# A two-layer attention and SwiGLU kernel: QKV projections staged through DRAM with halo rows, attention cores rescheduled

## The chip, the cores and the metric

The kernel runs on one core of a Trainium2 chip. The metric is the device time of one execution in microseconds (us), as the median of several runs. Engines in the profile: PE is TensorE (PEld its weight loads), DVE is VectorE, ACT is ScalarE, POOL is GpSimd, SP is SyncE. In the traces an instruction that waits holds up those that stand behind it in its engine's queue. At 429 to 448 us of the kernel before (the chain further down) the multiplies of a core, L142, wait 8.09 and 3.20 us for shifted rows; three gate multiplies L206, whose inputs TensorE and ScalarE had finished by 440.5 us, stand behind them in VectorE's queue and start at 447.49, 449.22 and 450.42.

## The reference

Two layers, each of attention and an MLP, on a sequence of 2048 rows of 1024 numbers in bfloat16, with 32 heads of 32. Attention looks at 8 keys per row, at distances 0, 2, 4, ... 14.

```python
def attention(x, wqkv, wo):                 # W, dil = 8, 2
    q, k, v = split_heads(x @ wqkv)
    idx = pos[:, None] - arange(W)[None, :] * dil
    kg, vg = k[idx], v[idx]                 # 8 shifted copies of the rows; masked where idx < 0
    attn = softmax(where(mask, einsum("bhsd,bhswd->bhsw", q, kg) * Dh**-0.5, -1e9))
    return einsum("bhsw,bhswd->bhsd", attn, vg) @ wo
def mlp(x, w1, w3, w2):                     # F = 3584
    return (silu(x @ w1) * (x @ w3)) @ w2
for _ in range(2):
    x = x + attention(layernorm(x), wqkv, wo)
    x = x + mlp(layernorm(x), w1, w3, w2)
```

## The kernel before

The rows are cut into 4 blocks of 512, so there are 8 stages (layer, block). Each partition holds 4 neighbouring rows of one parity. The attention of a stage is done in 4 groups of 8 heads: `q_unit` projects K, V and Q of a group on TensorE, ScalarE copies PSUM into a tile `U`, and DMAs shift K and V rows between partitions so that each partition also has the 7 rows ahead of its own ("halo"). `core` then does scores, softmax and the weighted sum on VectorE, some 23 us for a group. The cores of block i+1 are written into the gate and up matmuls of block i.

```python
CFG = dict(n_pairs=2, NW=8, NU=3, NT=3, q_pos=(0, 2, 4, 6))
...
def q_unit(i, g, xT):
    b = i % NB
    U = work.tile([P, UE, UC], BF16, name="U", tag="U", bufs=cfg["NU"])
    for part, e0 in ((1, K0 + HALO), (2, V0 + HALO), (0, Q0)):
        ...                                     # matmuls into psq (2 PSUM buffers)
        nc.scalar.copy(out=U[:, e0 + 2 * jp:e0 + 2 * jp + 2, :], in_=ps[:])
    kv = U[:, 0:2 * KE, :].rearrange("p (t e) c -> p t e c", t=2)
    for h0 in (0, 64):                          # own rows of partition p-1 and p-2 become p's halo
        nc.scalar.dma_start(out=kv[h0 + 1:h0 + 64, :, 3:7, :], in_=kv[h0:h0 + 63, :, 7:11, :])
        nc.scalar.dma_start(out=kv[h0 + 2:h0 + 64, :, 0:3, :], in_=kv[h0:h0 + 62, :, 8:11, :])
    ...                                         # halo of the block's first partitions: carry, through DRAM
    return U

def core(i, g, U, o):                           # VectorE, with one Exp on ScalarE
    for w in range(W):                          # L142
        nc.vector.tensor_tensor(out=prod[:, w, :]..., in0=U[:, Q0:Q0 + C, :],
                                in1=U[:, K0 + HALO - w:K0 + HALO - w + C, :], op=ALU.mult)
    ...                                         # tree of adds, mask, max, subtract
    nc.scalar.activation(out=ex[:], in_=lg[:], func=ACTF.Exp, scale=float(DH) ** -0.5)
    ...                                         # sum, reciprocal, V multiplies, tree into o

def f_gu(i, xT, hT, fp):                        # gate and up of 256 columns
    ...                                         # 8 matmuls into pg (L200), 8 into pu (L203)
        nc.scalar.activation(out=sg[:], in_=pg[:], func=ACTF.Silu)
        nc.vector.tensor_tensor(out=hT[:, ft, :], in0=pu[:], in1=sg[:], op=ALU.mult)   # L206

for i in range(NS):
    o_proj(i, otile.pop(i))
    xf = ln_T(b)
    for fp in range(FT // 2):
        if i + 1 < NS and g < NG and fp == cfg["q_pos"][g]:
            U = q_unit(i + 1, g, xq[i + 1])
            core(i + 1, g, U, otile[i + 1])     # directly behind its projection
            g += 1
        f_gu(i, xf, hT, fp)
    if i + 2 < NS:
        xq[i + 2] = ln_T((i + 2) % NB)
    f_w2(i, hT, last=(i >= NS - NB))
```

Tiles have dependencies tracked for them, and a scheduler lays out each engine's queue from a model of durations; how early it places work behind a DMA seems to follow from what it thinks that DMA takes (run 2 bears on this; it was not tested by itself).

## Time and profile before

| | before |
|---|---|
| median of the runs | 2055.3 us (16 runs, 2047.8 to 2063.0) |
| span of the profiled run | 2052.6 us |
| mean granted TensorE clock | 0.93 |
| TensorE busy, VectorE busy | 84%, 51% |
| VectorE waiting for shifted rows | 266.2 us |

A line of the waits view names an engine, the instruction that waited and what it waited for; then us in total, times and the longest one. These lines of the kernel before are from it:

```profile
DVE prod L142 <- DMA U<-U: 266.2, 57, 11.5
...
PE pmm L200 <- DVE hT L206: 160.3, 27, 8.5
```

Fifty-seven waits, none over 11.5 us: the cores stand again and again, a little each time. One such chain, from the chain of work that ended last (start, length, what):

```profile
429.13 14.09 DMA U<-U
...
443.35 1.91 DVE prod L142 x3
...
447.49 0.69 DVE hT L206
...
448.23 3.57 PE pmm L200 x8
```

Read it downward: the shift lands, the core's multiplies start, the gate multiply L206 that stands behind them in VectorE's queue runs, and only then does TensorE get a PSUM buffer for the next gate matmuls, which take 3.57 us for eight, where an undisturbed group takes 1.89 us: about half the clock (granted 0.50 from 448.23 to 451.80 us, 1.00 from 315.34 to 350 us).

### The profile page before, as it was taken

How to read it: one execution, taken by the hardware profiler on the slowest of the kernel's cores; microseconds unless marked ns; L12 is line 12 of the kernel's file. 1: busy time of each engine (PE TensorE's matmuls, PEld its weight loads, DVE VectorE, ACT ScalarE, POOL GpSimd, SP SyncE). 2: the span in 40 equal slices, each digit the busy share in tenths (PEclk: the TensorE clock that was granted, in tenths of full speed). 3: DMA queues.
4: the chain of work that ended last, by engine and by line, in shares of the span. 5: the costliest groups of instructions: out<-in, count | busy, mean ns of one | idle time of the engine just before them, and what ended most of it. 6: DMA issues, size and time to landing. Idle time of an engine off the chain costs nothing.

```text
span 2052.6 us, 23292 instructions
## 1 busy us (share of the span) xinstructions
PE 1728.7 (84%) x9570; PEld 943.3 (46%) x9728; DVE 1048.7 (51%) x1562; ACT 457.7 (22%) x646; POOL 2.2 (0%) x9
## 2 busy tenths in 40 slices
PE   5618879987899878997889978898879978798998
PEld 4504534454445444454534545344544455444443
DVE  3885764256724567135861477515764246723111
ACT  2203222032211322122211322203222022211210
POOL 0000000000000000000000000000000000000000
PEclk9859989999899998999999989999989999999999
DMA  9403544445444444444454445444554544545452
GB/s 219 122 19 111 163 128 144 143 125 146 132 153 144 132 138 126 149 140 133 135 148 146 140 125 150 136 149 139 151 140 134 156 139 134 145 154 155 135 154 81
DMA packets 430715, 282.96 MB, mean 138 GB/s; under 512 B 8624, under 2 KB 418128, under 8 KB 430608
## 3 DMA queue, kind: packets, MB, share of 16 engines
q1 hardware_dynamic: 413184, 251.69, 42.7%
q10 hardware_dynamic: 17424, 29.77, 4.7%
q8 instruction: 76, 1.25, 0.2%
q14 instruction: 31, 0.25, 0.0%
HBM read 248.12 MB, written 4.60 MB: 123 GB/s over the span
## 4 chain that ended last, share of the span: by engine, by line
PE 63%; DMA 21%; DVE 9%; ACT 3%; issue 2%; ACTq 1%; SPq 0%; DVEq 0%
DMA U<-U 20%; PE pmm L217 19%; PE pmm L200 14%; PE psq L121 12%; PE pmm L203 11%; PE psq L188 5%; DVE prod L142 3%; DVE prod L147 2%; PE pt L107 1%; ACT U L123 1%; DVE hT L206 1%; ACT tT L108 1%; DVE prod L167 1%; ACT tT L182 1%; ACTq L134 1%
## 5 line engine op out<-in xcount | busy, mean ns | idle before, releaser
L200 PE MATMUL pmm<-tT,wpg 128*128 128x512 bf16 x1732 | 460.6, 406 | 186.2 <-DVE hT L206 160.3
L203 PE MATMUL pmm<-tT,wpg 128*128 128x512 bf16 x1749 | 432.6, 387 | 2.0
L121 PE MATMUL psq<-wpg,tT 128*128 128x256 bf16 x3072 | 366.8, 280 | 47.1 <-ACT U L123 47.1
L217 PE MATMUL pmm<-wpg,hT 128*128 128x512 bf16 x1753 | 388.0, 379 | 2.1
L200 PEld LDWEIGHTS <-wpg 128*128 128x128 bf16 x1792 | 182.8, 102 | 412.2 <-issue 233.7
L121 PEld LDWEIGHTS <-tT 128*128 128x128 bf16 x3072 | 308.3, 101 | 107.1 <-issue 50.7
L142 DVE TENSOR_TENSOR prod<-U 128x1024 bf16<-128x1024 bf16 x256 | 162.3, 687 | 353.3 <-DMA U<-U 266.2
L203 PEld LDWEIGHTS <-wpg 128*128 128x128 bf16 x1792 | 179.8, 100 | 225.3 <-issue 28.4
L217 PEld LDWEIGHTS <-hT 128*128 128x128 bf16 x1792 | 174.6, 98 | 207.2
L206 DVE TENSOR_TENSOR hT<-pmm,sg 128x512 bf16<-128x512 f32 x224 | 154.0, 687 | 216.5 <-PE pmm L203 198.4
L205 ACT ACTIVATE sg<-pmm 128x512 bf16<-128x512 f32 x224 | 131.6, 597 | 590.5 <-PE pmm L200 555.9
L221 DVE TENSOR_TENSOR x_sb<-pmm,x_sb 128x512 bf16<-128x512 f32 x64 | 44.3, 692 | 348.4 <-PE pmm L217 348.4
L123 ACT CAST U<-psq 128x512 bf16<-128x512 f32 x192 | 110.4, 585 | 268.8 <-PE psq L121 251.1
L167 DVE TENSOR_TENSOR prod<-U,a 128x1024 bf16<-128x1024 bf16 x256 | 157.0, 685 | 1.1
L147 DVE TENSOR_TENSOR prod<-prod 128x4096 bf16<-128x4096 bf16 (+3 forms) x128 | 153.4, 1198 | 1.4
L188 PE MATMUL psq<-wpg,tT 128*128 128x512 bf16 x496 | 111.7, 380 | 0.6 <-issue 0.2
L182 ACT COPY tT<-pt 128x1024 bf16<-128x1024 bf16 x32 | 30.2, 1025 | 341.0 <-PE pt L181 341.0
L97 DVE BATCH_NORM_STATS2 st<-x_sb 128x6 f32<-128x512 bf16 x128 | 82.0, 673 | 8.3 <-DMA x_sb<-in_A_x_dram 7.5
L205 ACT ACT_TABLE_LOAD x42 | 53.9, 1283 | 129.2 <-DMA carry<-U 40.3
L188 PEld LDWEIGHTS <-tT 128*128 128x128 bf16 x512 | 49.7, 98 | 57.5 <-issue 1.1
L170 DVE TENSOR_TENSOR prod<-prod 128x4096 bf16<-128x4096 bf16 x32 | 73.3, 2290 | 0.9
L108 ACT COPY tT<-pt 128x1024 bf16<-128x1024 bf16 x64 | 61.0, 1020 | 31.4 <-PE pt L107 31.4
(31 smaller groups left out, 444.2 us busy)
## 6 DMA issues: line engine op xcount, KB each, us to landing
wpg<-in_B_w_dram SPq DMA_DIRECT2D x336, 512.0 KB
wpg<-in_A_wqkv_dram SPq DMA_DIRECT2D x96, 512.0 KB
wpg<-in_A_wo_dram SPq DMA_DIRECT2D x32, 512.0 KB
U<-U ACTq DMA_DIRECT2D x64, 252.0 KB
U<-U ACTq DMA_DIRECT2D x64, 186.0 KB
x_sb<-in_A_x_dram SPq DMA_DIRECT2D x8, 512.0 KB
out_dram<-x_sb SPq DMA_DIRECT2D x8, 512.0 KB
carry<-U ACTq DMA_DIRECT2D x48, 8.0 KB
```

The source lines that it names most:

```text
L97: nc.vector.bn_stats(out=st[:, j, c, :], in_=x_sb[:, b * C + j, c * 512:(c + 1) * 512])
L121: nc.tensor.matmul(ps[:, jj, :], lhsT=xT[:, kt, j * P:(j + 1) * P], rhs=pg[:, kt, :], start=(kt == 0), stop=(kt == KT - 1))
L123: nc.scalar.copy(out=U[:, e0 + 2 * jp:e0 + 2 * jp + 2, :], in_=ps[:])
L142: nc.vector.tensor_tensor(out=prod[:, w, :].rearrange("p (j c) -> p j c", j=C), in0=U[:, Q0:Q0 + C, :], in1=U[:, K0 + HALO - w:K0 + HALO - ...
L147: nc.vector.tensor_tensor(out=pv[:, :, 0:n], in0=pv[:, :, 0:n], in1=pv[:, :, n:2 * n], op=ALU.add)
L167: nc.vector.tensor_tensor(out=pa[:, w, :].rearrange("p (g e t) -> p g e t", e=DH // 2, t=2), in0=U[:, V0 + HALO - w:V0 + HALO - w + C, :]. ...
L188: nc.tensor.matmul(ps[:], lhsT=oT[:, kt, j * P:(j + 1) * P], rhs=pgs[kt // 4][:, kt % 4, :], start=(kt == 0), stop=(kt == KT - 1))
L200: nc.tensor.matmul(pg[:], lhsT=w1p[:, kt, fi * P:(fi + 1) * P], rhs=xT[:, kt, :], start=(kt == 0), stop=(kt == KT - 1))
L203: nc.tensor.matmul(pu[:], lhsT=w3p[:, kt, fi * P:(fi + 1) * P], rhs=xT[:, kt, :], start=(kt == 0), stop=(kt == KT - 1))
L205: nc.scalar.activation(out=sg[:], in_=pg[:], func=ACTF.Silu)
L206: nc.vector.tensor_tensor(out=hT[:, ft, :], in0=pu[:], in1=sg[:], op=ALU.mult)
L217: nc.tensor.matmul(acc[j][:], lhsT=hT[:, ft, j * P:(j + 1) * P], rhs=pg[:, f4, :], start=(ft == 0), stop=(ft == FT - 1))
```

## The change

Its intent is to take the transfers of shifted rows off the path. The projections of all groups are written to DRAM (`kvd`, `qd`), and a group's K, V and halo come back with one wide load each, from three row offsets. The projection of a block is no longer tied to its cores: the four blocks of the first layer are projected up front, later ones in the tail of an MLP stage, three stages ahead. The cores get low priority, so that the scheduler spreads them among the gate multiplies. The diff, cut to its core:

```diff
+    kvd[(l, g)] = dram.tile([2, NCH, C * UC], BF16, ...)     # 4 leading rows of zeros
+    qd[(l, g)] = dram.tile([NB * P, C * UC], BF16, ...)
...
-                nc.scalar.copy(out=U[:, e0 + 2 * jp:e0 + 2 * jp + 2, :], in_=ps[:])
-        ... shifts U<-U and carries
+                nc.scalar.copy(out=stg[:, 2 * jp:2 * jp + 2, :], in_=ps[:])
+            src = stg[:].rearrange("p j c -> p (j c)")
+            if part == 0:
+                nc.scalar.dma_start(out=qd[(l, g)][b * P:(b + 1) * P, :], in_=src)
+            else:
+                nc.scalar.dma_start(out=kvd[(l, g)][part - 1, b * P + 4:(b + 1) * P + 4, :], in_=src)
+
+    def load_U(l, b, g):
+        U = work.tile([P, UE, UC], BF16, name="U", tag="U", bufs=cfg["NU"])
+        for t in range(2):
+            src = bass.AP(tensor=kv.tensor, offset=..., ap=[[row, P], [2 * row, 3], [1, row]])
+            nc.gpsimd.dma_start(out=U[:, t * KE:(t + 1) * KE, :]..., in_=src)
+        nc.gpsimd.dma_start(out=U[:, Q0:Q0 + C, :]..., in_=qd[(l, g)][b * P:(b + 1) * P, :])
...
+    def cores(s):
+        l, b = divmod(s, NB)
+        with tc.high_priority(offset=-cfg["bg"]):
+            otile[s] = work.tile([P, C, D], BF16, name="o", tag="o", bufs=cfg["NO"])
+            for g in range(NG):
+                U = load_U(l, b, g)
+                core(b, g, U, otile[s])
+
+    for b in range(NB):
+        xq = ln_T(b, per_tile=(b == 0))
+        for g in range(NG):
+            q_proj(0, b, g, xq)
+        if b == 0:
+            cores(0)
+    o_proj(0, otile.pop(0))
+    xf = ln_T(0)
     for i in range(NS):
...
+        if i + 1 < NS:
+            cores(i + 1)
+        if i >= 1 and (i - 1) + NB < NS:
+            xq2 = ln_T((i - 1) % NB)
         for fp in range(FT // 2):
-            if ...: U = q_unit(i + 1, ...); core(i + 1, ...)
-            f_gu(i, xf, hT, fp)
+            f_gu(xf, hT, fp)
+        if xq2 is not None:
+            for g in range(NG):
+                q_proj((i - 1) // NB + 1, (i - 1) % NB, g, xq2)
+        if i + 1 < NS:
+            o_proj((i + 1) % NB, otile.pop(i + 1))
+            xf = ln_T((i + 1) % NB)
+        f_w2(b, hT, last=(i >= NS - NB))
```

Also changed: neighbouring partitions now hold the two parities (the x loads step by two partitions), the first block's norm is done tile by tile, the output projection and norm of the next block move ahead of w2, and w_out pages are read once for all tiles.

More of the change, by code (lines that the diff above doesn't have):

```diff
@@ L25 @@
 NG = D // UC
-HALO = W - 1
-KE = HALO + C
+KE = 3 * C
+OWN = 2 * C
 K0, V0, Q0 = 0, KE, 2 * KE
 UE = 2 * KE + C
+NCH = 2 * (S // 2 // C) + 4
 EPS = 1e-5
 NEG = -1.0e9
-CFG = dict(n_pairs=2, NW=8, NU=3, NT=3, q_pos=(0, 2, 4, 6))
+CFG = dict(n_pairs=2, NW=8, NU=3, NT=3, NO=1, bg=4000)
 @with_exitstack
@@ L49 @@
     ps_tr = ctx.enter_context(tc.tile_pool(name="ps_tr", bufs=2, space=bass.MemoryType.PSUM))
-    ident = const.tile([P, P], BF16, name="ident")
-    make_identity(nc, ident[:])
-    mask = const.tile([P, W, C, HG], FP32, name="mask")
-    nc.gpsimd.memset(mask[:], 0.0)
-    for half in range(2):
-        sl = mask[half * 64:(half + 1) * 64]
-        nc.gpsimd.affine_select(out=sl, in_=sl, pattern=[[-1, W], [1, C], [0, HG]], compare_op=ALU.is_ge,
-                                fill=NEG, base=0, channel_multiplier=C)
-    x_sb = const.tile([P, NB * C, D], BF16, name="x_sb")
-    eps_t = const.tile([P, 1], FP32, name="eps_t")
-    nc.vector.memset(eps_t[:], EPS)
-    zero = const.tile([32, UC], BF16, name="zero")
-    nc.vector.memset(zero[:], 0.0)
-    zcarry = dram.tile([2, 2, 8, UC], BF16, name="zcarry")
-    nc.scalar.dma_start(out=zcarry[:].rearrange("a b e c -> (a b e) c"), in_=zero[:])
-    carry = {}
     xin = A_x[0].rearrange("(b q j two) d -> b two q j d", b=NB, q=64, j=C, two=2)
@@ L74 @@
     w2_v = B_w2.rearrange("(f p) n -> p f n", p=P)
+    x_sb = const.tile([P, NB * C, D], BF16, name="x_sb")
+    for b in range(NB):
+        for par in range(2):
+            nc.sync.dma_start(out=x_sb[par:P:2, b * C:(b + 1) * C, :], in_=xin[b, par])
+    zero = const.tile([64, 64], BF16, name="zero")
+    nc.vector.memset(zero[:], 0.0)
+    kvd = {}
+    qd = {}
+    for l in range(n_pairs):
+        for g in range(NG):
+            kvd[(l, g)] = dram.tile([2, NCH, C * UC], BF16, name=f"kvd{l}_{g}")
+            qd[(l, g)] = dram.tile([NB * P, C * UC], BF16, name=f"qd{l}_{g}")
+            for t in range(2):
+                nc.gpsimd.dma_start(out=kvd[(l, g)][t, 0:4, :].rearrange("r (s c) -> (r s) c", c=64), in_=zero[:])
+    ident = const.tile([P, P], BF16, name="ident")
+    make_identity(nc, ident[:])
+    eps_t = const.tile([P, 1], FP32, name="eps_t")
+    nc.vector.memset(eps_t[:], EPS)
+    mask = const.tile([P, W, C, HG], FP32, name="mask")
+    with tc.tile_pool(name="tmp", bufs=1) as tmp:
+        m0 = tmp.tile([64, W, C, HG], FP32, name="m0")
+        nc.gpsimd.memset(m0[:], 0.0)
+        nc.gpsimd.affine_select(out=m0[:], in_=m0[:], pattern=[[-1, W], [1, C], [0, HG]], compare_op=ALU.is_ge,
+                                fill=NEG, base=0, channel_multiplier=C)
+        for par in range(2):
+            nc.gpsimd.dma_start(out=mask[par:P:2], in_=m0[:])
     def page_cols(view, c0):
@@ L84, in page_rows, with ln_T @@
         return pg
-    for b in range(NB):
-        for par in range(2):
-            nc.sync.dma_start(out=x_sb[par * 64:(par + 1) * 64, b * C:(b + 1) * C, :], in_=xin[b, par])
-    def ln_T(b):
+    def ln_T(b, per_tile=False):
         xT = work.tile([P, KT, TB], BF16, name="tT", tag="tT", bufs=cfg["NT"])
@@ L94, in ln_T, with stats @@
         rs = work.tile([P, C], FP32, name="rs", tag="rs")
-        for j in range(C):
+        def stats(j):
             for c in range(2):
@@ L98, in ln_T, with rstd, norm @@
             nc.vector.bn_aggr(out=mv[:, j, :], in_=st[:, j, :, :])
-        nc.scalar.activation(out=rs[:], in_=mv[:, :, 1], func=ACTF.Sqrt, bias=eps_t[:, 0:1])
-        nc.vector.reciprocal(out=rs[:], in_=rs[:])
-        for j in range(C):
+        def rstd(j0, j1):
+            nc.scalar.activation(out=rs[:, j0:j1], in_=mv[:, j0:j1, 1], func=ACTF.Sqrt, bias=eps_t[:, 0:1])
+            nc.vector.reciprocal(out=rs[:, j0:j1], in_=rs[:, j0:j1])
+        def norm(j):
             xn = work.tile([P, D], BF16, name="xn", tag="xn")
@@ L108, in ln_T, with q_proj @@
             nc.scalar.copy(out=xT[:, :, j * P:(j + 1) * P], in_=pt[:])
-        return xT
-    def q_unit(i, g, xT):
-        b = i % NB
-        U = work.tile([P, UE, UC], BF16, name="U", tag="U", bufs=cfg["NU"])
-        for part, e0 in ((1, K0 + HALO), (2, V0 + HALO), (0, Q0)):
+        if per_tile:
+            for j in range(C):
+                stats(j); rstd(j, j + 1); norm(j)
+        else:
+            for j in range(C):
+                stats(j)
+            rstd(0, C)
+            for j in range(C):
+                norm(j)
+        return xT
+    def q_proj(l, b, g, xT):
+        for part in (1, 2, 0):
             pg = page_cols(wqkv_v, part * D + g * UC)
+            stg = work.tile([P, C, UC], BF16, name="stg", tag="stg", bufs=3)
             for jp in range(C // 2):
@@ L122, in q_unit, with core @@
                                          start=(kt == 0), stop=(kt == KT - 1))
-                nc.scalar.copy(out=U[:, e0 + 2 * jp:e0 + 2 * jp + 2, :], in_=ps[:])
-        kv = U[:, 0:2 * KE, :].rearrange("p (t e) c -> p t e c", t=2)
-        for h0 in (0, 64):
-            nc.scalar.dma_start(out=kv[h0 + 1:h0 + 64, :, 3:7, :], in_=kv[h0:h0 + 63, :, 7:11, :])
-            nc.scalar.dma_start(out=kv[h0 + 2:h0 + 64, :, 0:3, :], in_=kv[h0:h0 + 62, :, 8:11, :])
-        src = zcarry if b == 0 else carry[(i - 1, g)]
-        nc.scalar.dma_start(out=kv[0:P:64, :, 0:7, :], in_=src[:, :, 1:8, :])
-        nc.scalar.dma_start(out=kv[1:P:64, :, 0:3, :], in_=src[:, :, 5:8, :])
-        if b < NB - 1:
-            cr = dram.tile([2, 2, 8, UC], BF16, name=f"carry{i}_{g}")
-            carry[(i, g)] = cr
-            nc.scalar.dma_start(out=cr[:, :, 0:4, :], in_=kv[62:P:64, :, 7:11, :])
-            nc.scalar.dma_start(out=cr[:, :, 4:8, :], in_=kv[63:P:64, :, 7:11, :])
-        return U
-    def core(i, g, U, o):
-        b = i % NB
+                nc.scalar.copy(out=stg[:, 2 * jp:2 * jp + 2, :], in_=ps[:])
+            src = stg[:].rearrange("p j c -> p (j c)")
+            if part == 0:
+                nc.scalar.dma_start(out=qd[(l, g)][b * P:(b + 1) * P, :], in_=src)
+            else:
+                nc.scalar.dma_start(out=kvd[(l, g)][part - 1, b * P + 4:(b + 1) * P + 4, :], in_=src)
+    def load_U(l, b, g):
+        U = work.tile([P, UE, UC], BF16, name="U", tag="U", bufs=cfg["NU"])
+        kv = kvd[(l, g)]
+        row = C * UC
+        for t in range(2):
+            src = bass.AP(tensor=kv.tensor, offset=kv.offset + (t * NCH + b * P) * row, ap=[[row, P], [2 * row, 3], [1, row]])
+            nc.gpsimd.dma_start(out=U[:, t * KE:(t + 1) * KE, :].rearrange("p (r j) c -> p r (j c)", r=3), in_=src)
+        nc.gpsimd.dma_start(out=U[:, Q0:Q0 + C, :].rearrange("p j c -> p (j c)"), in_=qd[(l, g)][b * P:(b + 1) * P, :])
+        return U
+    def core(b, g, U, o):
         prod = work.tile([P, W, C * UC], BF16, name="prod", tag="prod", bufs=1)
@@ L142, in core @@
             nc.vector.tensor_tensor(out=prod[:, w, :].rearrange("p (j c) -> p j c", j=C), in0=U[:, Q0:Q0 + C, :],
-                                    in1=U[:, K0 + HALO - w:K0 + HALO - w + C, :], op=ALU.mult)
+                                    in1=U[:, K0 + OWN - w:K0 + OWN - w + C, :], op=ALU.mult)
         pv = prod[:].rearrange("p w (g d) -> p (w g) d", d=DH)
@@ L148, in core @@
             n //= 2
-        NL = W * C * HG
         lg = work.tile([P, W, C * HG], FP32, name="lg", tag="lg")
@@ L167, in core @@
             nc.vector.tensor_tensor(out=pa[:, w, :].rearrange("p (g e t) -> p g e t", e=DH // 2, t=2),
-                                    in0=U[:, V0 + HALO - w:V0 + HALO - w + C, :].rearrange("p j (h e t) -> p (j h) e t", e=DH // 2, t=2),
+                                    in0=U[:, V0 + OWN - w:V0 + OWN - w + C, :].rearrange("p j (h e t) -> p (j h) e t", e=DH // 2, t=2),
                                     in1=a2[:, w, :, :].unsqueeze(2).to_broadcast([P, C * HG, DH // 2, 2]), op=ALU.mult)
@@ L173, in core, with o_proj @@
                                 in1=pa[:, 1, :].rearrange("p (j c) -> p j c", j=C), op=ALU.add)
-    def o_proj(i, o):
-        b = i % NB
+    def o_proj(b, o):
         oT = work.tile([P, KT, TB], BF16, name="tT", tag="tT", bufs=cfg["NT"])
@@ L182, in o_proj @@
             nc.scalar.copy(out=oT[:, :, j * P:(j + 1) * P], in_=pt[:])
-        for ch in range(2):
-            pgs = [page_rows(wo_v, 4 * kh, ch * 512) for kh in range(2)]
-            for j in range(C):
+        pgs = [[page_rows(wo_v, 4 * kh, ch * 512) for kh in range(2)] for ch in range(2)]
+        for j in range(C):
+            for ch in range(2):
                 ps = ps_qo.tile([P, 512], FP32, name="psq", tag="psq")
                 for kt in range(KT):
-                    nc.tensor.matmul(ps[:], lhsT=oT[:, kt, j * P:(j + 1) * P], rhs=pgs[kt // 4][:, kt % 4, :],
+                    nc.tensor.matmul(ps[:], lhsT=oT[:, kt, j * P:(j + 1) * P], rhs=pgs[ch][kt // 4][:, kt % 4, :],
                                      start=(kt == 0), stop=(kt == KT - 1))
@@ L191, in o_proj, with f_gu @@
                 nc.vector.tensor_tensor(out=xs, in0=ps[:], in1=xs, op=ALU.add)
-    def f_gu(i, xT, hT, fp):
+    def f_gu(xT, hT, fp):
         w1p = page_cols(w1_v, fp * 256)
@@ L206, in f_gu, with f_w2 @@
             nc.vector.tensor_tensor(out=hT[:, ft, :], in0=pu[:], in1=sg[:], op=ALU.mult)
-    def f_w2(i, hT, last):
-        b = i % NB
+    def f_w2(b, hT, last):
         for ch in range(2):
@@ L223, in f_w2 @@
             for par in range(2):
-                nc.sync.dma_start(out=xout[b, par], in_=x_sb[par * 64:(par + 1) * 64, b * C:(b + 1) * C, :])
-    xq = {0: ln_T(0)}
-    otile = {0: work.tile([P, C, D], BF16, name="o", tag="o", bufs=2)}
-    for g in range(NG):
-        U = q_unit(0, g, xq[0])
-        core(0, g, U, otile[0])
-    if NS > 1:
-        xq[1] = ln_T(1 % NB)
+                nc.sync.dma_start(out=xout[b, par], in_=x_sb[par:P:2, b * C:(b + 1) * C, :])
+    otile = {}
+    def cores(s):
[5 more added lines that the diff above has]
+                core(b, g, U, otile[s])
+    for b in range(NB):
+        xq = ln_T(b, per_tile=(b == 0))
[5 more added lines that the diff above has]
+    xf = ln_T(0)
     for i in range(NS):
-        b = i % NB
-        o_proj(i, otile.pop(i))
-        xf = ln_T(b)
+        l, b = divmod(i, NB)
         hT = work.tile([P, FT, TB], BF16, name="hT", tag="hT", bufs=1)
         if i + 1 < NS:
-            otile[i + 1] = work.tile([P, C, D], BF16, name="o", tag="o", bufs=2)
-        g = 0
+            cores(i + 1)
+        xq2 = None
+        if i >= 1 and (i - 1) + NB < NS:
+            xq2 = ln_T((i - 1) % NB)
         for fp in range(FT // 2):
-            if i + 1 < NS and g < NG and fp == cfg["q_pos"][g]:
-                U = q_unit(i + 1, g, xq[i + 1])
-                core(i + 1, g, U, otile[i + 1])
-                g += 1
-            f_gu(i, xf, hT, fp)
-        if i + 2 < NS:
-            xq[i + 2] = ln_T((i + 2) % NB)
-        f_w2(i, hT, last=(i >= NS - NB))
+            f_gu(xf, hT, fp)
+        if xq2 is not None:
+            for g in range(NG):
+                q_proj((i - 1) // NB + 1, (i - 1) % NB, g, xq2)
[3 more added lines that the diff above has]
+        f_w2(b, hT, last=(i >= NS - NB))
 _INS = ['A_x', 'A_wqkv', 'A_wo', 'B_x', 'B_w1', 'B_w3', 'B_w2']
```

## The prediction

> **What bounds the kernel now.** I read the page first (busy shares and the 40 slices), then the chain that ended last, then the groups, then the timeline of TensorE in one stage.
>
> ```profile
> PE 1728.7 (84%) x9570; PEld 943.3 (46%) x9728; DVE 1048.7 (51%) x1562; ACT 457.7 (22%) x646; POOL 2.2 (0%) x9
> ...
> PEclk9859989999899998999999989999989999999999
> ...
> PE 63%; DMA 21%; DVE 9%; ACT 3%; issue 2%; ACTq 1%; SPq 0%; DVEq 0%
> ```
>
> TensorE is the busiest engine, but only 63% of the chain is its work: 21% is DMA, and the by-line row under it puts 20% on U<-U, the shift of K and V rows between partitions. A DMA stands in the chain only if work waits for it. The groups say who does:
>
> ```profile
> L200 PE MATMUL pmm<-tT,wpg 128*128 128x512 bf16 x1732 | 460.6, 406 | 186.2 <-DVE hT L206 160.3
> L142 DVE TENSOR_TENSOR prod<-U 128x1024 bf16<-128x1024 bf16 x256 | 162.3, 687 | 353.3 <-DMA U<-U 266.2
> L206 DVE TENSOR_TENSOR hT<-pmm,sg 128x512 bf16<-128x512 f32 x224 | 154.0, 687 | 216.5 <-PE pmm L203 198.4
> ```
>
> The attention core on VectorE (L142) waits 266.2 us for U<-U, the gate multiply (L206) stands behind it in the same in-order queue, and the gate matmul (L200) waits 160.3 us for L206 to free its PSUM buffer. So a late DMA stops TensorE through two in-order queues. Timeline of TensorE in the first stage (start, us, ..., idle before):
>
> ```profile
> 233.83 3.57 PE L200 MATMUL pmm<-tT,wpg 128*128 128x512 bf16 x8 [5.06 <-DVE hT L206]
> ...
> 267.19 3.57 PE L200 MATMUL pmm<-tT,wpg 128*128 128x512 bf16 x8 [5.52 <-DVE hT L206]
> ...
> 303.21 3.57 PE L200 MATMUL pmm<-tT,wpg 128*128 128x512 bf16 x8 [6.33 <-DVE hT L206]
> ...
> 315.34 1.89 PE L200 MATMUL pmm<-tT,wpg 128*128 128x512 bf16 x8
> 317.06 1.89 PE L203 MATMUL pmm<-tT,wpg 128*128 128x512 bf16 x8
> ```
>
> One stop per head group; after it, eight matmuls take 3.57 us (half clock); undisturbed, groups of eight start 1.725 us apart, 215.7 ns per matmul. The start is worst, as no MLP work exists yet beside block 0's cores. Windows of 50 us (PE, PEld, DVE, ACT, POOL busy, clock, DMA share, GB/s):
>
> ```profile
> 100.00:150.00 50.00, 2.07 (x18) 1.23 (x16) 46.20 (x62) 2.69 (x5) 0.00 (x0) 0.55 0.10 29
> 350.00:400.00 50.00, 49.04 (x248) 23.26 (x252) 5.53 (x8) 3.42 (x4) 0.00 (x0) 1.00 0.47 147
> ```
>
> The first shows TensorE empty while VectorE works alone; the second what a full TensorE looks like: clock 1.00, weights at 147 GB/s.
>
> **TensorE's floor.** N=512: 5376+512 = 5888 x 215.7 ns = 1270 us. N=256 (QKV): 3072 x 109 ns (48 in 5.25 us in the chain) = 335 us. Transposes: 768 x about 57 ns = 44 us. Sum about 1650 us; the span is 2052.6, so 403 us are idle or at half clock, close to the chain's 20.4% for U<-U (419 us).
>
> [...] 1.725 us per eight, 3.57 us after each 5 to 6 us stop. [...] the x loads into half tiles ran at 222 to 223 GB/s, the weights behind them at 290 to 294. [...]
>
> **The change part by part.**
>
> (1) U<-U and carries go. Instead each K, V, Q part is stored to DRAM (3 parts x 32 units = 96 stores of 256 KB, 25 MB) and U is loaded with its halo by GpSimd (K and V 768 KB each, Q 256 KB, 1.8 MB x 32 = 59 MB). About 30 MB of shifts leave, so traffic goes from 283 to about 335 MB: near 190 GB/s over a 1760 us span. The trace moved 290 GB/s at its fullest, so it fits on average.
>
> (2) All four layer-0 projections are done first, and later ones a stage or more ahead; cores run at low priority. A load of U then has tens of us of slack (three U buffers, one core 23.2 us). The built program's order shows cores spread between the gate multiplies, not in front of them. This removes the 266.2 us wait, and with it most of the 160.3 us and the half clock. VectorE work is unchanged: one core is 8x0.687 + 4.8 + 8x0.685 + 2.29 + 1.22 + 0.69 + 3.2 of small operations = 23.2 us; a stage has four (93), 28 gate multiplies (19), 16 residual adds (11) and one or two layer norms (8.5 each): 132 to 140 us. TensorE needs 164 us per stage, 206 with a projection. TensorE bounds.
>
> (3) The start. I expect the first QKV near 27 us (25.9 before). The first core needs three projections (11 us), a store and a load[...]: near 47 us. In the order the norm of block 2 stands inside the fourth core: 47 + 3x24 + 8 = 127 us on VectorE, while TensorE arrives at 27 + 84 = 111 us; it waits 16 us (partly sooner, as each Exp stands before PSUM copies in ScalarE's queue). Then two blocks of QKV (2x42) and their transposes: output projection at about 215 us. Projection 16 us, then norm and transposes with nothing else for TensorE, 14 us: the MLP starts at 245 us.
>
> (4) From there the remaining TensorE work is 1650 less 168 (QKV), 8 (norm transposes), 16 (projection) and 2: 1456 us, so 1701 us with no stop, and 8 us for the last adds and stores (TensorE ends at 2044.6 of 2052.6 now): 1709 us.
>
> (5) New stops. Between gate multiplies the order places 3.7 to 3.8 us of VectorE work where cores run, against TensorE's 3.45 us; PSUM gives about 5 us of slack. Stages 0 and 1 have no projection to catch up in: first gate of stage 0 to the thirteenth of stage 1 is 223 us of VectorE against 208 of TensorE: 10 us lost. Seven output projections: an add, a core multiply and a norm statistic per tile, 2.1 against 1.73 us: 2.5 us each, 17. Seven norms behind them: about 2 us each, 14. w2 drains and U arrivals: 10. Sum about 50. **1760 us.**
>
> **Rivals.** (a) GpSimd's loads come late[...]: the wait L142 <- U<-U returns as U<-kvd. For it: a load is four times the bytes of a shift and every load goes through an engine new to this. Against: loads are issued up to two cores ahead[...]. If each of 32 cores waited 5 us, half hidden: 1840. (b) VectorE's queue becomes the bound: its order comes from a model, and if it is some 5% too dense all along, 7 stages x 10 us more: 1830. For it: segments of 5.0 to 5.7 us in the order; against: VectorE is idle in the second half of stages 1 to 5. (c) DMA contention: while projections and cores overlap[...]. Then TensorE waits for weights at the start: 20 to 40 us, 1790. (d) Transfers were hidden anyway: refuted by the chain's 20%.
>
> **Range and chances.** The floor of start, 1650 and tail is 27+1650+8 = 1685, so under 1715 all would have to be hidden; (a), (b), (c) give 1790 to 1840. Range 1715 to 1835. Missing 2% (2015) would need more than 250 us of new waits: faster 0.98.
>
> **What would show it right or wrong.** Right: L164 (core multiply) idle for DMA under 60 us; L220 (gate) idle for L226 under 70; granted clock 0.97 or more; DMA gone from the chain save at the start; first gate matmul at 235 to 260 us; about 335 MB moved; GpSimd's loads never the releaser of a long wait in the middle. Wrong: waits on U<-kvd above 100 us (a), TensorE idle spread over all gate groups (b), TensorE idle for weight pages or PSUM copies behind a stage store (c), or a first gate matmul past 290 us.

The sum on record was 1760 us, with one cut term in it: in (3), about 9 us for a store and a load, an estimate given without its numbers, which leads from 27 and 11 to the 47 us and so into the 245 and the 1760. TensorE's paces are those of the trace: from 315.34 to 342.96 us 16 groups of eight start 1.726 us apart.

## The result, and the profile after

The changed kernel takes **1748.0 us** (median of 8 runs, 1744.1 to 1749.5) against 2055.3 us, and its output is correct. The ratio is 0.8502, 95% interval 0.8489 to 0.8515. (Ratios here are the mean time of one kernel's fast runs over that of the other's of the same rounds, so not quite the ratio of the medians quoted.) From the page of the changed kernel: engines, granted clock by slice, bytes moved, and the chain by engine.

```profile
PE 1666.4 (95%) x9597; PEld 926.7 (53%) x9728; DVE 1039.1 (60%) x1565; ACT 432.5 (25%) x624; POOL 76.5 (4%) x122
...
PEclk9899999999999999999999999999999999999999
...
DMA packets 443564, 337.36 MB, mean 193 GB/s; under 512 B 11040, under 2 KB 412704, under 8 KB 443456
...
PE 64%; DVE 30%; ACT 2%; DMA 2%; issue 2%; SPq 0%; POOL 0%; DVEq 0%; POOLq 0%; ACTq 0%
```

VectorE does the same work (1039 us against 1049) and TensorE is busy at 95%. DMA fell from 21% of the chain to 2%, although more bytes move (337.36 MB against 282.96). The groups that answer to the three shown before (line numbers differ: L220 is the gate matmul, L164 the core's first multiply, L226 the gate multiply):

```profile
L220 PE MATMUL pmm<-tT,wpg 128*128 128x512 bf16 x1751 | 424.4, 382 | 14.5 <-DVE x_sb L240 11.8
...
L226 DVE TENSOR_TENSOR hT<-pmm,sg 128x512 bf16<-128x512 f32 x224 | 154.1, 688 | 308.4 <-PE pmm L223 296.2
...
L164 DVE TENSOR_TENSOR prod<-U 128x1024 bf16<-128x1024 bf16 x256 | 161.9, 680 | 19.4 <-DMA U<-qd 18.8
```

The core waits 19.4 us for its inputs in place of 353.3 (266.2 of that for the shifts, 77.7 for PSUM copies), and the gate matmul 14.5 in place of 186. VectorE now waits for TensorE (308.4 us), as it should where TensorE bounds. The core's wait that is left is a single one, at the start, as the waits view shows:

```profile
POOL U L157 <- DVE prod L188: 1135.0, 27, 124.1
...
DVE prod L164 <- DMA U<-qd: 18.8, 1, 18.8
...
PE psq L142 <- ACT stg L144: 16.0, 4, 10.1
```

GpSimd, which issues the loads, stands 1135 us at full U buffers: the loads are ready to go before there is room. The same two windows as before (PE, PEld, DVE, ACT, POOL busy, clock, DMA share, GB/s):

```profile
100.00:150.00 50.00, 44.24 (x401) 38.72 (x400) 48.11 (x67) 17.73 (x29) 4.07 (x6) 0.97 0.85 269
350.00:400.00 50.00, 48.73 (x257) 23.38 (x260) 47.99 (x74) 9.57 (x11) 2.03 (x3) 1.00 0.60 191
```

In the first, TensorE was at 2.07 us before. In the second both engines are nearly full.

**Where the 307 us came from.** In the kernel before, the first w2 matmul is at 349.65 us, and the dense TensorE work done until then is about 202 us: some 148 us lost. In the changed kernel TensorE reaches the first gate matmul at 251.45 us after about 192 us of dense work: 59 lost. (Both sums of dense work are estimates from the paces in the prediction.) So the start gave about 88 us. From one w2 to the next, a stage took 246 to 249 us before (349.65, 595.43, 844.34). In the changed kernel a stage without a projection takes about 170 us, those with one 211.6 (517.57 to 729.15). The rest, about 220 us, came from the stages.

### The profile page after: what moved, and what is told of

Its sections match the earlier page's. It is cut to its first block, busy times and chain, and to the rows that moved or that the text cites. A ratio compares the mean times of both kernels' runs of the same rounds, so it can differ in the third digit from the quotient of the medians.

```text
span 1745.3 us, 23469 instructions
## 1 busy us (share of the span) xinstructions
PE 1666.4 (95%) x9597; PEld 926.7 (53%) x9728; DVE 1039.1 (60%) x1565; ACT 432.5 (25%) x624; POOL 76.5 (4%) x122
## 2 busy tenths in 40 slices
DMA packets 443564, 337.36 MB, mean 193 GB/s; under 512 B 11040, under 2 KB 412704, under 8 KB 443456
## 3 DMA queue, kind: packets, MB, share of 16 engines
q10 hardware_dynamic: 13824, 25.17, 3.8%
## 4 chain that ended last, share of the span: by engine, by line
PE 64%; DVE 30%; ACT 2%; DMA 2%; issue 2%; SPq 0%; POOL 0%; DVEq 0%; POOLq 0%; ACTq 0%
PE pmm L223 21%; PE pmm L220 21%; PE psq L142 13%; DVE prod L164 6%; PE pmm L236 6%; DVE prod L169 5%; DVE prod L188 5%; DVE st L106 3%; DVE prod L191 2%; DVE x_sb L211 2%; DVE x_sb L240 1%; PE psq L208 1%; DVE prod L192 1%; PE pt L119 1%; ACT tT L120 1%
## 5 line engine op out<-in xcount | busy, mean ns | idle before, releaser
L220 PE MATMUL pmm<-tT,wpg 128*128 128x512 bf16 x1751 | 424.4, 382 | 14.5 <-DVE x_sb L240 11.8
L223 PE MATMUL pmm<-tT,wpg 128*128 128x512 bf16 x1757 | 421.5, 380 | 2.8 <-DVE x_sb L240 0.8
L142 PE MATMUL psq<-wpg,tT 128*128 128x256 bf16 x3072 | 343.6, 275 | 16.5 <-ACT stg L144 16.0
L226 DVE TENSOR_TENSOR hT<-pmm,sg 128x512 bf16<-128x512 f32 x224 | 154.1, 688 | 308.4 <-PE pmm L223 296.2
L142 PEld LDWEIGHTS <-tT 128*128 128x128 bf16 x3072 | 303.4, 99 | 55.7 <-issue 17.3
L220 PEld LDWEIGHTS <-wpg 128*128 128x128 bf16 x1792 | 175.3, 98 | 225.2 <-issue 19.0
L223 PEld LDWEIGHTS <-wpg 128*128 128x128 bf16 x1792 | 175.7, 98 | 213.2 <-issue 4.0
L164 DVE TENSOR_TENSOR prod<-U 128x1024 bf16<-128x1024 bf16 x256 | 161.9, 680 | 19.4 <-DMA U<-qd 18.8
L144 ACT CAST stg<-psq 128x512 bf16<-128x512 f32 x192 | 112.0, 585 | 219.9 <-PE psq L142 218.0
L193 DVE TENSOR_TENSOR o<-prod 128x1024 bf16<-128x1024 bf16 x32 | 22.0, 686 | 231.7 <-PE pt L201 231.1
L157 POOL DMA_DIRECT2D U<-kvd x64 | 47.6, 744 | 1210.7 <-DVE prod L188 1135.0
L208 PEld LDWEIGHTS <-tT 128*128 128x128 bf16 x512 | 49.4, 98 | 56.6
L119 PE MATMUL pt<-ident,xn 128*128 128x128 bf16 x512 | 41.4, 235 | 34.7 <-DVE xn L115 33.5
```

The lines of the kernel that those rows point to most:

```text
L142: nc.tensor.matmul(ps[:, jj, :], lhsT=xT[:, kt, j * P:(j + 1) * P], rhs=pg[:, kt, :], start=(kt == 0), stop=(kt == KT - 1))
L144: nc.scalar.copy(out=stg[:, 2 * jp:2 * jp + 2, :], in_=ps[:])
L164: nc.vector.tensor_tensor(out=prod[:, w, :].rearrange("p (j c) -> p j c", j=C), in0=U[:, Q0:Q0 + C, :], in1=U[:, K0 + OWN - w:K0 + OWN - w ...
L208: nc.tensor.matmul(ps[:], lhsT=oT[:, kt, j * P:(j + 1) * P], rhs=pgs[ch][kt // 4][:, kt % 4, :], start=(kt == 0), stop=(kt == KT - 1))
L220: nc.tensor.matmul(pg[:], lhsT=w1p[:, kt, fi * P:(fi + 1) * P], rhs=xT[:, kt, :], start=(kt == 0), stop=(kt == KT - 1))
L223: nc.tensor.matmul(pu[:], lhsT=w3p[:, kt, fi * P:(fi + 1) * P], rhs=xT[:, kt, :], start=(kt == 0), stop=(kt == KT - 1))
```

## The experiments

All 12 outputs but that of `after_nocore` are correct. I had three theories of the main gain. DISTANCE: what cost was that a core is asked for directly behind the projection that feeds it. TRANSPORT: the wide loads through DRAM are what is faster than 64-partition shifts. PRIORITY: the low priority of the cores is what spreads them. Later, two theories of what sets the end of the start.

**1. DRAM staging kept, distance taken away.** Each group's projection goes back to directly ahead of its core, at the places that the kernel before used.

```diff
+    def unit(n, g, xq, o):
+        q_proj(l, b, g, xq); U = load_U(l, b, g); core(b, g, U, o)
...
-        if i + 1 < NS:
-            cores(i + 1)
         for fp in range(FT // 2):
+            if i + 1 < NS and g < NG and fp == (0, 2, 4, 6)[g]:
+                unit(i + 1, g, xq[i + 1], otile[i + 1]); g += 1
             f_gu(xf, hT, fp)
```

> The changed kernel with its DRAM staging and its loads, but the projections put back where the kernel before has them: each head group's projection directly ahead of its core, inside the MLP of the block before, core at ordinary priority. Theory DISTANCE (the gain comes from loading U long before its core is due): the wait returns as core multiply <- U<-qd, some 8 to 12 us per head group, 150 to 330 us over the run, and the time goes back to 1950 to 2080 us. Rival TRANSPORT (store plus load through DRAM is simply quicker or cheaper than the shift between partitions): at most 1850 us.

Measured: 1967.8 us (ratio to before 0.9577, 0.9548 to 0.9606), so 220 us of the 307 are lost again, inside what DISTANCE expected and far above the 1850 of TRANSPORT. Its waits and the window of the start:

```profile
DVE prod L164 <- DMA U<-qd: 206.0, 29, 27.6
```

```profile
100.00:150.00 50.00, 4.71 (x30) 3.29 (x32) 42.71 (x57) 4.68 (x6) 0.00 (x0) 0.51 0.00 0
```

The wait is back as U<-qd, now longer each time (up to 27.6 us), since a round trip is a store and a load (those of Q land in 5.5 and 4.7 us at the median); the start is empty again. Stages take 236.8 us. So DRAM staging without distance keeps about 88 us, together with the stride-two partitions and the shared w_out pages, which this run keeps too. The 220 us that went are not distance alone: the run also puts the output projection and norm back behind w2.

**2. Partition shifts kept, cores called later.** In the kernel before, each core is called two gate steps behind its projection.

```diff
-                U = q_unit(i + 1, g, xq[i + 1])
-                core(i + 1, g, U, otile[i + 1])
+                pend.append((g, q_unit(i + 1, g, xq[i + 1])))
...
+            if pend and fp == cfg["q_pos"][pend[0][0]] + 2:
+                gg, U = pend.pop(0)
+                core(i + 1, gg, U, otile[i + 1])
```

> The kernel before with its partition shifts kept and no DRAM staging, but each core called two MLP steps (about 14 us of gate and up matmuls) after its projection, so that the shift has time. Theory DISTANCE: the core's wait for U<-U (266 us) falls below 100 us and the time to 1790 to 1900 us; the start of the run stays as bad as before, so it does not reach 1748. Rival TRANSPORT: the shifts still block ScalarE's queue and arrive late, 1980 to 2060 us.

Measured: 1971.8 us (0.9585, 0.9557 to 0.9613), outside of what DISTANCE expected and a little under what the rival expected.

```profile
DVE prod L142 <- DMA U<-U: 185.1, 56, 11.1
...
PE pmm L200 <- DVE hT L206: 73.5, 25, 7.8
```

The 185.1 us show that no distance was made: there are still 56 waits. In the timeline most of a projection ran at 443.8 to 451.9 us, its shifts were issued at 449 to 455, and the core that uses them still began at 458.4, directly behind the core before it. Calling a core later in the program did not make it later in the queue here; presumably the scheduler put it where its model thought the rows would be there, which was not looked at. So this run decides nothing between the theories.

**3. Partition shifts kept, with real distance.** Three of the next block's four groups are projected ahead of the previous block's w2, into the three U buffers; the cores are called in the next stage.

```diff
+        us[i + 2] = [q_unit(i + 2, g, xq[i + 2]) for g in range(3)]     # ahead of f_w2
         f_w2(i, hT, last=(i >= NS - NB))
...
-                U = q_unit(i + 1, g, xq[i + 1])
-                core(i + 1, g, U, otile[i + 1])
+            if i + 1 < NS and fp in (0, 2, 4, 6):
+                g = fp // 2
+                core(i + 1, g, us[i + 1][g], otile[i + 1])
+                if g == 0:
+                    us[i + 1].append(q_unit(i + 1, 3, xq[i + 1]))
```

> The kernel before with its partition shifts kept (no staging through DRAM), but with real distance: the projections of groups 0 to 2 of the next block are made ahead of the previous block's w2, into three U buffers, and the cores are called during the gate and up of the next block. DISTANCE (what costs is that a core is asked for directly behind the projection that feeds it): the 266 us that VectorE waits for the shifted rows fall below 60 us, the stages after the first shorten from 246 us to 205-220 us, the start stays as it was, total 1800-1880 us. TRANSPORT (the DRAM staging with its wide loads is what is faster, whatever the order): the wait stays above 130 us and the total above 1930 us.

Measured: 1904.0 us (0.9251, 0.9235 to 0.9267), between the two expectations; the wait fell to 135.3 us, not below 60, and is just on TRANSPORT's side of the expected lines (above 130). In the timeline of TensorE, the stage from 383.5 to 618.6 us (235 us) has one long stop left in its gate matmuls, and three at the new place:

```profile
438.67 3.29 PE L200 MATMUL pmm<-tT,wpg 128*128 128x512 bf16 x8 [7.04 <-DVE hT L206]
...
545.59 8.89 PE L121 MATMUL psq<-wpg,tT 128*128 128x256 bf16 x80 [0.78 <-ACT U L123]
...
557.64 3.53 PE L121 MATMUL psq<-wpg,tT 128*128 128x256 bf16 x16 [2.94 <-ACT U L123]
...
564.97 6.78 PE L121 MATMUL psq<-wpg,tT 128*128 128x256 bf16 x48 [3.58 <-ACT U L123]
```

Distance without any change of transport gave 155 us, half of the gain, and this although ScalarE's PSUM copies now wait behind carry and shift DMAs in its queue (72.1 and 47.4 us in the waits). Each projection held in advance occupies a U buffer here; there are three, and the four blocks of the first layer cannot be held at all. DRAM had room for all of them: the changed kernel stores 25.17 MB there. The waits that are left stand where a core still is directly behind its own projection: the fourth group's (10.20 us at 430.37) and the first of the next block, which the scheduler pulled forward (9.00 us at 548.39, 4.59 at 555.47). The two cores behind it, at 575.46 and 600.83, run their eight multiplies without a wait. So the run has distance for some cores only, and it is those that do not wait: DISTANCE is supported, though its numbers were not met. That DRAM staging matters mostly because it makes room for distance is the reading that fits runs 1 and 3; no run has full distance with the old shifts. Staging without distance (run 1) gave 88 us, so neither part alone explains the 307.

**4. Distance of two stages in place of three.** In the changed kernel, two blocks are projected up front, not four, and the others in the stages' tails, two stages ahead.

```diff
-    for b in range(NB):
+    for b in range(2):
...
-        if i >= 1 and (i - 1) + NB < NS:
-            xq2 = ln_T((i - 1) % NB)
+        if i + 2 < NS:
+            xq2 = ln_T((i + 2) % NB)
```

> The changed kernel with two blocks of projection in the start in place of four; the other units are projected two stages ahead in the stages' tails, six times in place of four. If the four blocks up front are what keeps TensorE at work beside the first cores: TensorE has nothing to do in about 110-147 us (about 38 us) and the total grows to 1755-1785 us. If they only move work: within 5 us of 1748 us.

Measured: 1826.1 us (0.8874, 0.8848 to 0.89), 78 us longer than the changed kernel and far past the expected 1755 to 1785. TensorE's timeline in the start and in the first two stages:

```profile
145.23 0.61 PE L201 MATMUL pt<-ident,o 128*128 128x128 bf16 x4 [19.16 <-DVE o L193]
...
314.82 16.20 PE L142 MATMUL psq<-wpg,tT 128*128 128x256 bf16 x128 [10.64 <-ACT stg L144]
...
536.46 16.32 PE L142 MATMUL psq<-wpg,tT 128*128 128x256 bf16 x128 [9.69 <-ACT stg L144]
```

The expected stop is there but is 19 us, not 38, as TensorE comes late to it. What I had not expected are the 10 us stops in every projection, each followed by a slower stretch (128 matmuls in 16.2 us where 14 is the undisturbed time, at 109 ns each; the granted clock is 0.97 in the mean of 250 to 450 us). A stage takes 221.7 us (400.08 to 621.79) in place of 211.6. The cause is again a core put directly behind its own projection: GpSimd's loads wait for the stores of that projection (1125.4 us in 54 waits for those of K and V), VectorE waits 174.6 us in seven waits of up to 27 us, and ScalarE's Exp of that core stands ahead of the PSUM copies of the projection. Six stages of 10 us more each are about 60 us, and the start adds about 14: together most of the 78. So "a stage ahead" is not enough where the tail of one stage touches the next.

**5. Priority.** `bg=4000` becomes `bg=0` in the changed kernel.

> The changed kernel without the low priority of the cores (offset 0 in place of 4000). Theory DISTANCE: with U long there, priority is a detail; the built order still puts gate multiplies between core operations, segments a little longer, 1745 to 1790 us. Rival PRIORITY (keeping the cores behind the MLP in VectorE's queue is what frees TensorE): the gate matmuls wait for the gate multiply again, 100 us or more in total, 1850 us or more.

Measured: 1747.2 us (0.8494, 0.8477 to 0.8512), the same as the changed kernel within the intervals. PRIORITY is refuted: the low priority does nothing that these runs can tell.

**6. The cores taken out.** A core is replaced by one copy of Q into `o`.

```diff
-        prod = work.tile(...) ... nc.vector.tensor_tensor(out=o[:, :, g * UC:(g + 1) * UC], ...)
+        nc.vector.tensor_copy(out=o[:, :, g * UC:(g + 1) * UC], in_=U[:, Q0:Q0 + C, :])
```

> Wrong result on purpose: the changed kernel with each core replaced by one copy of Q into o, all loads, stores and matmuls kept. It measures what all of VectorE's core work costs in the changed kernel. Theory (TensorE bounds, the cores cost only the start and a few us per stage): 1680 to 1705 us, that is 45 to 70 us less than 1748, of which about 25 at the start. Rival (VectorE's queue or the DMA traffic is the hidden bound): if VectorE, below 1670; if DMA contention, no lower than 1730.

Measured: 1696.5 us in one run (so its state is unknown), inside what the theory expected. VectorE's busy time falls from 1039.1 to 378.0 us; these 661 us of work cost the changed kernel 51 us of time. Its first gate matmul is at 224.61 us, so 27 of the 51 lie in the start. In its window from 50 to 100 us:

```profile
50.00:100.00 50.00, 50.00 (x460) 44.82 (x459) 1.71 (x4) 16.88 (x29) 9.50 (x14) 1.00 1.07 361
```

TensorE is full and 361 GB/s move, so neither the weights nor the stores hold it up in the start.

**7. The loads on another queue.** The changed kernel's loads of U are issued by SyncE, whose queue also holds the weight pages: `nc.gpsimd.dma_start` becomes `nc.sync.dma_start` in three lines.

> The changed kernel with its loads of projected rows issued from SyncE's queue, ahead of and between the weight pages, in place of GpSimd's queue. If the queue matters (GpSimd stands 1135 us at a full U buffer[...]): the weight pages behind the blocked loads come late, TensorE waits for wpg rise from 0.5 us to over 60 us, total 1800-1950 us. Rival (queue choice is free): within 1 per cent of 1748 us and TensorE's waits for wpg below 5 us.

Measured: 1740.3 us in one run (state unknown, as it is single). The theory that the queue matters is refuted: TensorE has no wait for weights in the list, and SyncE stands only 76.6 us before full U buffers, at most 5.5 us at once. But it is 8 us faster, more than the spread of the changed kernel's runs, which I had not expected. The landing times are alike (7.0 us against 7.1 for K and V), and the first core multiply is at 52.91 us against 52.77. What differs is one stop of TensorE. First the line of the changed kernel, then that of this run:

```profile
65.74 43.52 PE L142 MATMUL psq<-wpg,tT 128*128 128x256 bf16 x384 [10.10 <-ACT stg L144]
```

```profile
65.94 43.49 PE L142 MATMUL psq<-wpg,tT 128*128 128x256 bf16 x384 [3.88 <-ACT stg L144]
```

The stop is 6.2 us shorter, and the span 6.8 us. On ScalarE, the scheduler had put the first core's Exp four PSUM copies later (behind the 18th, not the 14th; TensorE, with its two buffers, gets 20 and 16 groups of matmuls done before it stops). In both, the Exp starts at 64.8 to 64.9 us, when VectorE has its logits; every copy behind it waits, and with two PSUM buffers TensorE waits too.

**8. That Exp moved by itself.** This tests two theories of the start. TENSORE-START: it ends when TensorE has done its work and its stops. START-CHAIN: it ends when VectorE's chain of cores has. The Exp gets a bias of zero, made from the 22nd PSUM copy, so that it cannot stand ahead of that copy. The loads stay on GpSimd.

```diff
+            if (l, b, g, part) == (0, 0, NG - 1, 2):
+                nc.scalar.mul(late[:], stg[:, C - 1, 0:1], 0.0)
...
         nc.scalar.activation(out=ex[:], in_=lg[:], func=ACTF.Exp, scale=float(DH) ** -0.5,
+                             **({"bias": late[:, 0:1]} if (b, g) == (0, 0) else {}))
```

> The changed kernel, its loads left on GpSimd, with one thing moved: the first core's Exp is given a bias of zero that is made from the 22nd PSUM copy, so that ScalarE's queue cannot hold it ahead of that copy (it stood ahead of the 17th). TENSORE-START (the start's end is set by TensorE and the sum of its stops, and the 10.1 us stop is six PSUM copies standing behind an Exp that waits for VectorE): the stop at 55-66 us falls below 3 us, the first core multiply stays at 52-54 us, the MLP begins at 241-244 us, total 1737-1742 us. START-CHAIN (VectorE's cores set the start's end): the stop goes, the MLP start and the total stay within 3 us of 251 and 1748.

Measured: 1742.4 us (0.8466, 0.8448 to 0.8485; the changed kernel's interval is 0.8489 to 0.8515), span 1738.0. TensorE's timeline there:

```profile
33.98 35.09 PE L143 MATMUL psq<-wpg,tT 128*128 128x256 bf16 x320 [0.59 <-DMA wpg<-in_A_wqkv_dram]
...
244.10 1.89 PE L224 MATMUL pmm<-tT,wpg 128*128 128x512 bf16 x8 [0.64 <-ACT tT L121]
```

The stop is gone, the first core multiply is at 52.14 us (0.6 earlier), the MLP begins at 244.10 in place of 251.45. The median is 5.6 us lower, 0.4 us short of what was expected. (The expectation counts copies by TensorE's groups: in ScalarE's queue the Exp stood behind the 14th copy.) START-CHAIN is refuted, and the trace of the changed kernel says the same: at the end of its start VectorE stands idle for 47 us until TensorE has read the output tile `o`.

```profile
226.90 0.69 DVE L193 TENSOR_TENSOR o<-prod 128x1024 bf16<-128x1024 bf16 x1 [47.05 <-PE pt L201]
```

One reserve: the scheduler laid out some later transposes anew as well, and a new wait of 4.76 us appeared at 117 us, so the 10 us did not come back in full.

**9. The first core earlier.** Block 0 of x is loaded alone first, the others behind the first weight pages, and Q is projected, stored and loaded ahead of K and V.

```diff
-    for b in range(NB):            # x loads
+    load_x(0)                      # blocks 1 to 3 follow behind groups of block 0
...
-        for part in (1, 2, 0):
+        for part in (0, 1, 2):
```

> The changed kernel with the first block of x loaded alone first and the other blocks behind the first weight pages, and Q projected, stored and loaded ahead of K and V. START-CHAIN (the start is a chain of VectorE that begins with the first landed rows, so each us earlier of the first core multiply is a us off the total): first core multiply at 41-46 us instead of 52.8, total 1736-1742 us. Rival (TensorE or weight pages bound the start): the first multiply moves, the total stays within 3 us of 1748 us.

Measured: 1738.6 us (0.8445, 0.8432 to 0.8458), as START-CHAIN expected; the first multiply is at 40.98 us, 11.8 earlier, for 9.4 us of time. But this does not prove that theory, as the run changes two things at once: with the first block loaded alone, TensorE's first QKV matmul also starts at 16.68 us in place of 25.40, and the MLP at 243.48 in place of 251.45. Eight us earlier at both ends is what TENSORE-START expects too. TensorE's stop in the first block is 6.84 us in place of 10.10, but it is no longer the Exp's. On ScalarE:

```profile
41.82 0.30 ACT L112 ACTIVATE rs<-mv,eps_t 128x4 f32<-128x4 f32 x1 [8.90 <-DVE mv L109]
...
57.84 0.42 ACT L181 ACTIVATE ex<-lg 128x256 f32<-128x256 f32 x1 [0.57 <-DVE lg L179]
```

The Exp waits 0.57 us only. What now stands ahead of the PSUM copies is the square root of a later norm (L112). It waits 8.90 us for a statistic that stands in VectorE's queue behind the first core's multiply, which in turn waits 11.23 us for its rows. It is the same kind of stop with another instruction in front.

**10 to 12. Stops filled.** On top of run 9, the norm of the next block is called earlier, one group of block 2's projection is kept to fill the wait for the first block's norm, and block 3's projection moves out of the start into the first stage's tail.

```diff
-    for b in range(NB):
+    for b in range(3):             # the last group of block 2 comes behind o_proj(0) and its norm
...
-        if i >= 1 and (i - 1) + NB < NS:
+        if (i - 1) + NB < NS:
```

> The early Q version, with layer norm of the next block emitted earlier, and block 3's projection moved from the start into the first MLP stage's tail, so that TensorE does in the start only what the first block needs and later stops are filled. If the start is bound by VectorE's cores, moving the projection alone gains nothing and the sum is 1725-1738 us; if by TensorE, it gains up to 25 us more (below 1722 us); if the moved work meets VectorE's cores in stage 0 it loses: above 1745 us.

Measured: 1726.4 us (0.8386, 0.8373 to 0.8398). That is in the range expected if VectorE's cores bind the start, and not below the 1722 of TENSORE-START. The trace shows why neither fits alone: VectorE's wait for `o` at the end of the start is 1.40 us (at 162.68 us) in place of 47.05, so with a block's projection taken out the two engines end the start nearly together. What each of the three edits gave was not measured by itself. The same with the loads on SyncE:

> The filled version (1726.4 us) with its loads on SyncE's queue. If the gain of the loads on SyncE (1740.3 against 1748) came only from where the scheduler put the first Exp, no further gain is owed: 1720-1730 us. If SyncE's queue is itself quicker for the loads: about 1718 us.

Measured: 1724.1 us (0.8379, 0.8361 to 0.8397); the two intervals overlap, so the queue itself gave nothing that these runs can tell. And with block 3's projection ahead of the first MLP in place of in its tail, on SyncE too:

> The same with block 3's projection ahead of the first MLP instead of in its tail. It fills the stop of output projection and norm (about 10 us) but takes nothing out of the start: 1720-1732 us, within 6 us of the filled version.

Measured: 1729.0 us (0.8404, 0.8386 to 0.8422). The best versions, `after_filled` and `after_filled_sp`, are 1.4% under the changed kernel (0.8386 and 0.8379 over 0.8502). The window of 50:100 has TensorE busy for 45.20 us in `after_filled` against 39.90, and its wait of 6.87 us for the norm ahead of the first MLP, which the changed kernel has at 246 us, is gone. The floor of the prediction, 1685 us, is 39 us away.

## Why the prediction was right or wrong

The prediction was right: 1760 us in a range of 1715 to 1835, measured 1748.0. By its steps:

- **What bounds the kernel** and **step (2)** were right. The wait for rows went (L164 idle 19.4 us, under the 60 given), the gate matmul no longer waits for L226 at all, and the clock is 0.989. (One transfer of rows, 6.76 us at 838 us, is still in the chain behind the start.) The low priority, which step (2) also names, does nothing (run 5). Runs 1, 3 and 4 support that this needs distance: with DRAM and no distance the time is 1967.8, with shorter distance 1826.1, with distance and no DRAM 1904.0.
- **Step (1)** was right: 337.36 MB against 335 predicted, in 96 stores and 96 loads.
- **Step (3), the start**, ended at 251.45 us against 245. The first QKV came at 25.40 (27) and the first core at 52.77 (47): the store took 7.76 us and the load 5.83, where I had put 9 for both. I also had VectorE as what TensorE waits for in the middle of the start, with the Exp as a side remark. Run 8 showed the side remark to be the larger part in the changed kernel: one Exp in ScalarE's queue stopped TensorE for 10.10 us. TensorE and VectorE then arrived at the norm of block 2 about together (128.4 and 130.4 us), and the 16 us wait that I counted was 1.82.
- **Step (4), the dense work.** TensorE ended at 1739.2 us. Less 251.45, and less about 20 us of stops, this leaves 1468 us where I counted 1456. Run 6, at a clock of 0.999, takes 1464 us from its first gate matmul (224.61) to its last w2 matmul (1688.66), some 4 of it waits, so the dense work is about 1460. About 5 us of the rest are matmuls at a lower clock behind three stops, as this one:

```profile
628.77 3.43 PE L220 MATMUL pmm<-tT,wpg 128*128 128x512 bf16 x8 [2.35 <-DVE x_sb L240]
```

  The others are at 1051.31 (3.16 us after a stop of 2.36) and 1262.73 (2.96 after 2.03). The granted clock in the three groups is 0.54, 0.57 and 0.61. In the kernel before it is 0.50 in groups behind stops of 5.06 to 6.33 us (at 233.83, 267.19 and 303.21 us); these three stops are shorter, and the clock fell all the same.
- **Step (5) is the term that was mis-sized**: "Sum about 50" was about 20. The parts: gate loops 0 (10), output projections 0.5 (17), norms 7.4 (14), w2 drains and arrivals 12.7 (10). The failing part is "an add, a core multiply and a norm statistic per tile, 2.1 against 1.73 us". I added durations of 0.68 us each. The timeline of VectorE in the first output projection shows that independent operations overlap (start, duration):

```profile
227.50 0.68 DVE L211 TENSOR_TENSOR x_sb<-psq,x_sb 128x512 bf16<-128x512 f32 x1
228.10 0.68 DVE L164 TENSOR_TENSOR prod<-U 128x1024 bf16<-128x1024 bf16 x1
228.70 0.69 DVE L106 BATCH_NORM_STATS2 st<-x_sb 128x6 f32<-128x512 bf16 x1
229.31 0.68 DVE L211 TENSOR_TENSOR x_sb<-psq,x_sb 128x512 bf16<-128x512 f32 x1
```

  They start 0.60 us apart, so three are 1.80 us, nearly TensorE's own pace of 1.73; TensorE waits 0.5 us in all its output projections, so the rest is hidden, presumably by the two PSUM buffers. The gate loops have no wait either; that the same overlap is the reason was not taken apart.
- **The sum**: start +6.5, dense +12, stops -30, tail -2 (6.1 in place of 8): 1760 - 13 = 1746 for the span, which is 1745.3. Errors of opposite sign cancelled in part, so that 1760 came this near is partly luck.
- **Rivals.** (a), GpSimd's loads late: refuted, one wait of 18.8 us, and run 7 shows the queue to be free (K and V land in 7.1 us at the median from GpSimd, with VectorE busy for up to 48.11 of 50 us, and in 7.0 us from SyncE). (b), VectorE too dense: refuted, L226 waits for TensorE. (c), contention: refuted, TensorE waits 0.5 us for weight pages; and 361 GB/s in run 6 show that the 290 I took as the fullest was no ceiling. (d) was refuted already.

What stays open: how much of the gain of run 1 belongs to the wide loads and how much to the other details that it keeps (stride-two partitions, w_out pages), and how much of the other 220 us belongs to the output projection and norm moved ahead of w2, was not taken apart. Of the stride-two partitions the trace shows one effect: between 5 and 10 us the DMA engines move 374 GB/s in place of 222, yet the first QKV matmul comes only 0.5 us earlier (25.40 against 25.88). About 3 us of the 12 us of extra dense work were not traced; some of TensorE's records are missing from the trace (9597 of 9728).

## What to carry to other kernels

When one engine's result goes to another through a DMA, look at how much other work lies between request and use, before trying a faster transfer: staging through DRAM moved more bytes (337.36 MB against 282.96), yet won, by the reading of runs 1 and 3, because it let projections run stages ahead without holding SBUF. Calling a consumer later in the program is not distance when a scheduler places it greedily (run 2), and distance that is just short shows up as a stop in another engine's queue (run 4). An activation that waits on a slow chain should not be queued ahead of PSUM copies that a matmul needs: one such Exp stopped TensorE for 10 us here, and when it was moved, 5.6 us of time came back (run 8); when it came early, another activation stood in its place (run 9).
